# An attention and MLP stack on one core: placing side work by a running clock, summing heads on PE for the first chunk, and starting the first attention early

## Chip, core and metric

One Trainium2 chip (trn2), one core. The metric is the device time of one execution in microseconds (us). Where kernels are compared, the ratio is the mean time of one kernel's fast runs over that of the kernel before in the same rounds, so it is not quite the ratio of the medians quoted.

Engine names: PE does matmuls, DVE is the vector engine, ACT the scalar engine, POOL the general engine, SP issues DMAs. PEld is PE's loading of weights.

Words used below: a unit of a projection, of WO or of W1 is eight matmuls of 128x512, about 1.73 us. A hole is a time in which PE stands idle; the profile shows it as a bracket behind the group that ends it. The granted clock is a share of PE's full clock; below 1.00 it is called cold here.

## The reference

S = 2048 rows of D = 1024, in bfloat16; two layers, each of an attention block and an MLP block with residuals.

```python
def _A_ref(x, wqkv, wo):              # H = 32 heads of 32; each row sees 8 rows, 2 apart
    qkv = (x @ wqkv)...               # q, k, v
    idx = pos[:, None] - arange(8) * 2
    logits = einsum("bhsd,bhswd->bhsw", q, k[idx]) * scale   # masked where idx < 0
    o = einsum("bhsw,bhswd->bhsd", softmax(logits), v[idx])
    return o @ wo
def _B_ref(x, w1, b1, w2, b2):        # F = 3584
    return gelu(x @ w1 + b1) @ w2 + b2

x = x + _A_ref(_layernorm(x)); x = x + _B_ref(_layernorm(x))     # twice
```

## The kernel before

The rows are cut into four chunks of 512, so two layers make eight chunk passes, called chunks 0 to 7 here. A pass goes: first layer norm (LN1) with PE transposes, Q, K and V projections, products q times shifted k on DVE, head sum by a matmul with a 0/1 matrix, softmax, broadcast of the weights back over the head's rows by matmul, PV (weights times shifted v) on DVE, WO with residual, second layer norm (LN2), W1 with gelu, W2 with residual. A chunk's attention runs beside the W1 and W2 of the chunk before it. Chunk 0 has no such neighbour.

The parts concerned, with cuts marked by `# ...` (the other comments are mine):

```python
q8 = const.tile([P, 8, C], BF, name="q8")       # one buffer each for q, k, v, weights, output
v8 = const.tile([P, 8, KROW], BF, name="v8")    # KROW = 14 rows of halo + 512
# ...
class QK:                                       # DVE: product, then running sum over dl
    def step(self, dl):
        prod = prodp.tile([P, W, C], BF, name="prod")
        nc.vector.tensor_tensor(out=prod, in0=q8[:, dl, :]..., in1=window(k8, dl), op=ALU.mult)
        if self.acc is None: self.acc = prod
        else: nc.vector.tensor_tensor(out=self.acc, in0=self.acc, in1=prod, op=ALU.add)
# ...
def pv():
    for dl in range(8):                         # all eight steps in one piece
        t = prodp.tile([P, W, C], BF, name="prod")
        nc.vector.tensor_tensor(out=t, in0=attn4, in1=window(v8, dl), op=ALU.mult)
        # three halving additions, the last one into o8[:, dl, :]
# ...
def wo_ln(i, tail_units):                       # LN2 transposes b(st), LNB_LAG = 3 counts later
    for it in seq:
        if it[0] == "wo":
            wo_unit(wt, xt, it[1], it[2])
            if it[2] == 1:
                last = a(it[1]); pend.append((cnt + LNB_LAG, it[1]))
        else: it[1]()
        cnt += 1
        while pend and pend[0][0] <= cnt: b(pend.pop(0)[1])
# ...
for n, u in enumerate(us):                      # chunk 0's projections, LN1 of chunk 1 at the front
    u()
    if n < ST: b1u(n)
red(); exp(); bc(0); bc(1); pv()                # chunk 0's attention
for u in qkv_units(1, xa.pop(1), None): u()     # all of chunk 1's projections
xb[0], last = wo_ln(0, [])                      # nothing beside chunk 0's LN2
# ...
side = {pr: [red], pe: [exp], p0: [lambda: bc(0)], p1: [lambda: bc(1), pv]}
```

The order of the program is only a priority: the compiler's scheduler orders each engine's instructions by it, from its own estimate of when inputs are ready.

## Time and profile before

| | before |
|---|---|
| median | 1337.57 us (4 runs, 1335.61 to 1339.78) |
| span of the profiled run | 1335.4 us |
| PE busy | 1278.9 us (96%) |
| DVE busy | 805.6 us (60%) |

PE is nearly always busy, so the profile is read by its holes: the last column of the PE timeline, idle time in brackets with what ended it. The prediction shows those lines. The shares by engine of the chain of waits that ended last:

```profile
PE 81%; DVE 10%; DMA 4%; POOL 3%; ACT 1%; issue 1%; POOLq 0%; SPq 0%; ACTq 0%
```

Only about half of the 10% of DVE is PV: that of chunk 0 gives 30 us and that of chunk 1 gives 34. From the DVE and POOL timelines (start, duration, engine, line, operation), the first and last piece of that PV and the halo copy after it:

```profile
78.39 4.50 DVE L260 TENSOR_TENSOR prod<-attn,v 128x4096 bf16<-128x4096 bf16 x2 [4.62 <-ACT attn L254]
...
111.93 0.76 DVE L263 TENSOR_TENSOR o<-prod 128x512 bf16<-128x512 bf16 x2
...
108.67 4.16 POOL L182 COPY v<-v 128x112 bf16<-128x112 bf16 x1 [46.69 <-DVE prod L260]
```

The reader should see that PV occupies DVE from 78.4 to 112.7, and that nothing in WO of chunk 0 or V of chunk 1 can pass it. In the chain of waits, the last V eviction before the long hole's end waits for the halo copy.

### The profile page before, as it was taken

The numbers are of one execution on the slowest core, as the hardware profiler recorded it, in microseconds if no ns is written. First come the engines' busy times: TensorE is split into PE (matmuls) and PEld (weight loads), VectorE is DVE, ScalarE is ACT, GpSimd is POOL, SyncE is SP. The second block draws the span as 40 slices with busy tenths as digits, with TensorE's granted clock in tenths as the row PEclk, the third lists the DMA queues.
The fourth block names the chain that finished last, engine by engine and source line by source line (L and its number), as shares of the span: only waits on it lengthen the run. The fifth ranks groups of instructions, "written<-read, shape, count | busy, mean of one in ns | idle before, by whom it ended". The sixth has DMA issues, their size and how long they took to land.

```text
span 1335.4 us, 18271 instructions
## 1 busy us (share of the span) xinstructions
PE 1278.9 (96%) x8064; PEld 828.5 (62%) x8064; DVE 805.6 (60%) x836; ACT 402.9 (30%) x648; POOL 191.2 (14%) x196
## 2 busy tenths in 40 slices
PE   6996899699999999999999999999999999999998
PEld 4663358555487655966469564785648765487477
DVE  6885967586573955559374691928739284574001
ACT  3341342033610344113531235202361034501310
POOL 3002300142011310023001420004201020003000
PEclk9998899899999999999999999999999999999999
DMA  8333354344555355463455534635444526453560
GB/s 291 136 112 115 111 141 144 108 144 168 164 156 179 110 203 142 142 241 114 140 143 180 191 119 157 164 132 186 165 144 132 205 79 213 119 174 128 180 166 32
DMA packets 186912, 202.77 MB, mean 152 GB/s; under 512 B 5456, under 2 KB 152912, under 8 KB 185808
## 3 DMA queue, kind: packets, MB, share of 16 engines
q1 hardware_dynamic: 186832, 201.60, 47.1%
q8 instruction: 63, 1.03, 0.3%
q14 instruction: 17, 0.14, 0.0%
HBM read 193.21 MB, written 8.39 MB: 151 GB/s over the span
## 4 chain that ended last, share of the span: by engine, by line
PE 81%; DVE 10%; DMA 4%; POOL 3%; ACT 1%; issue 1%; POOLq 0%; SPq 0%; ACTq 0%
PE ps L315 29%; PE ps L339 28%; PE ps L187 21%; DVE prod L260 3%; DVE stats L145 2%; DMA xmid<-xt 2%; PE ps L270 1%; PE pa L163 1%; DMA xt<-xmid 1%; DVE prod L261 1%; POOL rstd L150 1%; DVE xt L273 1%; DVE xn L152 1%; DMA out_dram<-xt 1%; POOL xt L325 1%; DVE prod L262 1%
## 5 line engine op out<-in xcount | busy, mean ns | idle before, releaser
L339 PE MATMUL ps<-wt,h 128*128 128x256 bf16 x3584 | 399.6, 273 | 10.3 <-DVE xt L342 10.3
L315 PE MATMUL ps<-xnT,wt 128*128 128x512 bf16 x1792 | 393.2, 380 | 0.3 <-ACT xnT L165 0.3
L339 PEld LDWEIGHTS <-h 128*128 128x128 bf16 x3584 | 350.4, 98 | 53.5 <-issue 10.9
L187 PE MATMUL ps<-xnT,wt 128*128 128x512 bf16 x1536 | 339.3, 382 | 11.1 <-ACT v L188 11.1
L315 PEld LDWEIGHTS <-wt 128*128 128x128 bf16 x1792 | 174.3, 98 | 213.7 <-issue 8.6
L187 PEld LDWEIGHTS <-wt 128*128 128x128 bf16 x1536 | 219.4, 144 | 124.5 <-issue 17.2
L318 ACT ACTIVATE h<-ps,b1t 128x512 bf16<-128x512 f32 x224 | 152.8, 689 | 197.5 <-PE ps L315 197.4
L165 ACT ACTIVATE xnT<-pa 128x512 bf16<-128x512 f32 x128 | 69.5, 595 | 442.4 <-PE pa L163 442.3
L342 DVE TENSOR_TENSOR xt<-ps,xt 128x512 bf16<-128x512 f32 x64 | 42.9, 688 | 258.7 <-PE ps L339 258.7
L260 DVE TENSOR_TENSOR prod<-attn,v 128x4096 bf16<-128x4096 bf16 x64 | 143.6, 2286 | 87.7 <-ACT attn L254 87.7
L200 DVE TENSOR_TENSOR prod<-q,k 128x4096 bf16<-128x4096 bf16 x64 | 152.3, 2409 | 6.3 <-ACT k L188 6.3
L205 DVE TENSOR_TENSOR prod<-prod 128x4096 bf16<-128x4096 bf16 x56 | 128.0, 2285 | 0.5
L270 PE MATMUL ps<-wt,o 128*128 128x512 bf16 x512 | 114.4, 379 | 0.0
L149 POOL TENSOR_SCALAR rstd<-mv 128x1 f32<-128x1 f32 x64 | 34.2, 535 | 497.3 <-DVE mv L147 496.8
L145 DVE BATCH_NORM_STATS2 stats<-xt 128x6 f32<-128x512 bf16 x128 | 84.7, 677 | 5.0 <-DMA xt<-in_A_x_dram 2.6
L270 PEld LDWEIGHTS <-o 128*128 128x128 bf16 x512 | 49.4, 98 | 55.1
L182 POOL COPY v<-v 128x112 bf16<-128x112 bf16 x6 | 24.9, 4155 | 374.3 <-DVE prod L260 374.3
L261 DVE TENSOR_TENSOR prod<-prod 128x2048 bf16<-128x2048 bf16 x64 | 75.3, 1219 | 0.0
L325 POOL TENSOR_TENSOR xt<-xt,b2bc 128x1024 bf16<-128x1024 bf16 x32 | 70.0, 2186 | 20.5 <-DVE xn L152 20.5
L163 PE MATMUL pa<-ident,xn 128*128 128x128 bf16 x512 | 43.4, 230 | 28.2 <-DVE xn L152 16.3
L188 ACT ACTIVATE v<-ps 128x512 bf16<-128x512 f32 x64 | 37.9, 597 | 86.0 <-PE ps L187 69.3
L163 PEld LDWEIGHTS <-xn 128*128 128x128 bf16 x512 | 34.6, 103 | 42.9 <-DVE xn L152 36.5
(49 smaller groups left out, 440.4 us busy)
## 6 DMA issues: line engine op xcount, KB each, us to landing
wt<-in_B_w_dram SPq DMA_DIRECT2D x64, 1792.0 KB, 8.1
wt<-in_A_wqkv_dram SPq DMA_DIRECT2D x24, 2048.0 KB, 8.6
wt<-in_A_wo_dram SPq DMA_DIRECT2D x8, 2048.0 KB, 7.8
xmid<-xt SPq DMA_DIRECT2D x4, 1024.0 KB, 10.5
xt<-xmid SPq DMA_DIRECT2D x4, 1024.0 KB, 5.5
out_dram<-xt SPq DMA_DIRECT2D x4, 1024.0 KB, 9.8
xt<-in_A_x_dram SPq DMA_DIRECT2D x3, 1024.0 KB, 7.0
xt<-in_A_x_dram SPq DMA_DIRECT2D x4, 256.0 KB, 3.5
```

The lines of the kernel that those rows point to most:

```text
L145: nc.vector.bn_stats(out=stats[:, hh, :], in_=xt[:, st, hh * 512:(hh + 1) * 512])
L163: nc.tensor.matmul(pt[:, j, :], lhsT=xn[:, kk * P:(kk + 1) * P], rhs=ident, start=True, stop=True)
L187: nc.tensor.matmul(pt, lhsT=ws[:, kk, dl, :], rhs=xnT[:, kk, :], start=(kk == 0), stop=(kk == KT - 1))
L200: ins = nc.vector.tensor_tensor(out=prod, in0=q8[:, dl, :].unsqueeze(1).to_broadcast([P, W, C]), in1=window(k8, dl), op=ALU.mult)
L205: nc.vector.tensor_tensor(out=self.acc, in0=self.acc, in1=prod, op=ALU.add)
L260: nc.vector.tensor_tensor(out=t, in0=attn4, in1=window(v8, dl), op=ALU.mult)
L261: nc.vector.tensor_tensor(out=t[:, 0:4, :], in0=t[:, 0:4, :], in1=t[:, 4:8, :], op=ALU.add)
L270: nc.tensor.matmul(pt, lhsT=o8[:, dl, st * P:(st + 1) * P], rhs=wt[:, dl, hf * 512:(hf + 1) * 512], start=(dl == 0), stop=(dl == 7))
L315: nc.tensor.matmul(pt, lhsT=wt[:, kk, j * P:(j + 1) * P], rhs=xnT[:, kk, :], start=(kk == 0), stop=(kk == KT - 1))
L318: nc.scalar.activation(out=h, in_=pt, func=AF.Gelu_apprx_tanh, bias=b1t[:, f:f + 1])
L325: nc.gpsimd.tensor_tensor(out=xt[:, st, :], in0=xt[:, st, :], in1=b2bc, op=ALU.add)
L339: nc.tensor.matmul(pt[:, s2, :], lhsT=hs[f][:, st * P:(st + 1) * P], rhs=wt[:, f, :], start=(f == 0), stop=(f == FT - 1))
```

## The change

The intent: give every piece of side work a time on a running clock instead of a position in a list of units; start chunk 0's attention while its V projection runs; take the head sum of chunk 0 off DVE by accumulating it in PSUM; cut PV into eight separately placed steps; put LN2's transposes four projection units after their input; keep three of chunk 1's V units back to stand beside chunk 0's LN2. The core of the diff, cut (lines with `@@` and the comment in it are mine):

```diff
-POS_RED, POS_EXP, POS_BC0, POS_BC1 = 6, 10, 15, 18
-LNB_LAG = 3
+T_MM = 1.73
+T_W2 = 6.13
+A_RED, A_EXP, A_BC0, A_BC1, A_PV, A_PVSTEP = 2.0, 8.0, 16.0, 19.5, 23.0, 4.3
+LNB_LAG = 5.0
@@ class QK
-            if self.acc is None:
+            if self.on_pe:
+                self.acc = prod            # red_pe(dl): eight matmuls, start=dl==0, stop=dl==7
+            elif self.acc is None:
@@ att_units
-        def pv():
-            for dl in range(8):
+        def pv(dl):
@@ new: Clock.at(t, fn), Clock.run(fn, dur): fn placed in front of the first unit starting at t or later
+    def sched_att(i, qk, t_ready):
+        red, exp, bc, pv = att_units(i, qk)
+        clk.at(t_ready + A_RED, red)
+        clk.at(t_ready + A_EXP, exp)
+        clk.at(t_ready + A_BC0, lambda: bc(0))
+        clk.at(t_ready + A_BC1, lambda: bc(1))
+        for dl in range(8):
+            clk.at(t_ready + A_PV + A_PVSTEP * dl, (lambda d: (lambda: pv(d)))(dl))
+    def run_wo(i, res):
+        ...
+            res["last"] = a(st)
+            clk.at(clk.t + 6.9, (lambda s_: (lambda: b(s_)))(st))
+    def sched_ln1(i, t0, lag=LNB_LAG):     # a(st) at t0 + 2.5 st, b(st) lag later
@@ prologue
+    qks[0] = QK(on_pe=True)
+    us0[0](); clk.t += T_MM
+    xts[1] = load_x(1)
+    xa[1] = sched_ln1(1, clk.t, 10.0)
+    for u in us0[1:]:
+        clk.run(u, T_MM)
+    sched_att(0, qks.pop(0), 16 * T_MM + 4.5 - 8.0)
+    for u in us1[:21]:
+        clk.run(u, T_MM)
+    clk.flush(1e9)
+    run_wo(0, r)
+    for u in us1[21:]:
+        clk.run(u, T_MM)
@@ loop (cut)
+        sched_att(j + 2, qks.pop(j + 2), clk.t + 2.0)
```

More of the change, by code (lines that the diff above doesn't have):

```diff
@@ L192, in load_qkv, with reduce_heads, __init__ @@
         return wt.rearrange("p k (m e) -> p k e m", e=8)
+    def reduce_heads(lg, src, start, stop):
+        for wh in range(2):
+            for sb in range(4):
+                nc.tensor.matmul(lg[wh][32 * sb:32 * sb + 32, :, :], lhsT=sel4,
+                                 rhs=src[:, wh * 4:(wh + 1) * 4, sb * P:(sb + 1) * P],
+                                 start=start, stop=stop, tile_position=(0, 32 * sb))
     class QK:
-        def __init__(self):
+        def __init__(self, on_pe=False):
             self.acc = None
+            self.on_pe = on_pe
+            self.lg = None
         def step(self, dl):
@@ L206, in step, with red_pe, u @@
             return ins
+        def red_pe(self, dl):
+            src = self.acc
+            def u():
+                if self.lg is None:
+                    self.lg = [pslg.tile([P, 4, P], F32, name="lg") for _ in range(2)]
+                reduce_heads(self.lg, src, dl == 0, dl == 7)
+            return u
     def att_units(i, qk):
@@ L212, in red @@
         def red():
-            acc = qk.acc
-            lg = [pslg.tile([P, 4, P], F32, name="lg") for _ in range(2)]
-            for wh in range(2):
-                for sb in range(4):
-                    nc.tensor.matmul(lg[wh][32 * sb:32 * sb + 32, :, :], lhsT=sel4,
-                                     rhs=acc[:, wh * 4:(wh + 1) * 4, sb * P:(sb + 1) * P],
-                                     start=True, stop=True, tile_position=(0, 32 * sb))
+            if qk.on_pe:
+                lg = qk.lg
+            else:
+                lg = [pslg.tile([P, 4, P], F32, name="lg") for _ in range(2)]
+                reduce_heads(lg, qk.acc, True, True)
             lgs = smx.tile([P, W, P], F32, name="lgs")
@@ L255, in bc @@
                                      func=AF.Copy)
-        def pv():
-            for dl in range(8):
-                t = prodp.tile([P, W, C], BF, name="prod")
-                nc.vector.tensor_tensor(out=t, in0=attn4, in1=window(v8, dl), op=ALU.mult)
-                nc.vector.tensor_tensor(out=t[:, 0:4, :], in0=t[:, 0:4, :], in1=t[:, 4:8, :], op=ALU.add)
-                nc.vector.tensor_tensor(out=t[:, 0:2, :], in0=t[:, 0:2, :], in1=t[:, 2:4, :], op=ALU.add)
-                nc.vector.tensor_tensor(out=o8[:, dl, :], in0=t[:, 0, :], in1=t[:, 1, :], op=ALU.add)
+        def pv(dl):
+            t = prodp.tile([P, W, C], BF, name="prod")
+            nc.vector.tensor_tensor(out=t, in0=attn4, in1=window(v8, dl), op=ALU.mult)
+            nc.vector.tensor_tensor(out=t[:, 0:4, :], in0=t[:, 0:4, :], in1=t[:, 4:8, :], op=ALU.add)
+            nc.vector.tensor_tensor(out=t[:, 0:2, :], in0=t[:, 0:2, :], in1=t[:, 2:4, :], op=ALU.add)
+            nc.vector.tensor_tensor(out=o8[:, dl, :], in0=t[:, 0, :], in1=t[:, 1, :], op=ALU.add)
         return red, exp, bc, pv
@@ L273, in wo_unit @@
         nc.vector.tensor_tensor(out=xs, in0=pt, in1=xs, op=ALU.add)
-    def wo_ln(i, tail_units):
-        xt = xts[i]
-        wt = load_w(A_wo.rearrange("(m e) n -> m e n", e=8), 8, D)
-        xnT, a, b = ln_units(xt)
-        main = []
-        for st in range(ST):
-            main.append(("wo", st, 0))
-            main.append(("wo", st, 1))
-        pend = []
-        cnt = 0
-        last = None
-        seq = main + [("tail", u) for u in tail_units]
-        for it in seq:
-            if it[0] == "wo":
-                wo_unit(wt, xt, it[1], it[2])
-                if it[2] == 1:
-                    last = a(it[1])
-                    pend.append((cnt + LNB_LAG, it[1]))
-            else:
-                it[1]()
-            cnt += 1
-            while pend and pend[0][0] <= cnt:
-                b(pend.pop(0)[1])
-        for _, st in pend:
-            b(st)
-        return xnT, last
     def w1_units(xnT, hs):
@@ L360, in u @@
                         qk.step(dl)
+                        if qk.on_pe:
+                            clk.at(clk.t + T_MM + 2.7, qk.red_pe(dl))
                 else:
@@ L372, in qkv_units @@
         return us
-    xa = {0: ln_all(xts[0])}
-    xts[1] = load_x(1)
-    late_consts()
-    qks = {0: QK(), 1: QK()}
-    us = qkv_units(0, xa.pop(0), qks[0])
-    xnT1, a1, b1u = ln_units(xts[1])
-    for st in range(ST):
-        a1(st)
-    for n, u in enumerate(us):
-        u()
-        if n < ST:
-            b1u(n)
-    xa[1] = xnT1
-    red, exp, bc, pv = att_units(0, qks[0])
-    red(); exp(); bc(0); bc(1); pv()
-    late_bias()
-    for u in qkv_units(1, xa.pop(1), None):
-        u()
@@ L392, with __init__, at, flush @@
-    xb = {}
-    xb[0], last = wo_ln(0, [])
-    first_qk = None
+    class Clock:
+        def __init__(self):
+            self.t = 0.0
+            self.q = []
+            self.n = 0
+        def at(self, t, fn):
+            self.q.append((t, self.n, fn))
+            self.n += 1
+            self.q.sort(key=lambda e: (e[0], e[1]))
+        def flush(self, t):
+            while self.q and self.q[0][0] <= t:
+                self.q.pop(0)[2]()
+        def run(self, fn, dur):
+            self.flush(self.t)
+            fn()
+            self.t += dur
@@ new lines @@
+    clk = Clock()
+    def sched_att(i, qk, t_ready):
[7 more added lines that the diff above has]
+    def run_wo(i, res):
+        xt = xts[i]
+        wt = load_w(A_wo.rearrange("(m e) n -> m e n", e=8), 8, D)
+        xnT, a, b = ln_units(xt)
+        res["xnT"] = xnT
+        for st in range(ST):
+            for hf in range(2):
+                clk.run(lambda: wo_unit(wt, xt, st, hf), T_MM)
+            res["last"] = a(st)
+            clk.at(clk.t + 6.9, (lambda s_: (lambda: b(s_)))(st))
@@ new lines, in sched_ln1 @@
+    def sched_ln1(i, t0, lag=LNB_LAG):
+        xnT, a, b = ln_units(xts[i])
+        for st in range(ST):
+            clk.at(t0 + 2.5 * st, (lambda s_: (lambda: a(s_)))(st))
+            clk.at(t0 + 2.5 * st + lag, (lambda s_: (lambda: b(s_)))(st))
+        return xnT
+    xa, xb, qks = {}, {}, {}
+    wq0 = None
+    xa[0] = ln_all(xts[0])
+    late_consts()
+    qks[0] = QK(on_pe=True)
+    us0 = qkv_units(0, xa.pop(0), qks[0])
+    us0[0]()
+    clk.t += T_MM
+    xts[1] = load_x(1)
+    xa[1] = sched_ln1(1, clk.t, 10.0)
@@ L395 @@
+    for u in us0[1:]:
+        clk.run(u, T_MM)
+    sched_att(0, qks.pop(0), 16 * T_MM + 4.5 - 8.0)
+    late_bias()
+    us1 = qkv_units(1, xa.pop(1), None)
+    for u in us1[:21]:
+        clk.run(u, T_MM)
+    clk.flush(1e9)
+    r = {}
+    run_wo(0, r)
+    for u in us1[21:]:
+        clk.run(u, T_MM)
+    clk.flush(1e9)
+    xb[0] = r["xnT"]
+    qks[1] = QK()
     for dl in range(8):
         ins = qks[1].step(dl)
-        if first_qk is None:
-            first_qk = ins
-    tc.add_manual_dep(first_qk.ins, last.ins.name,
-                      mybir.DependencyInfo(mybir.DependencyClass.NoSync, mybir.DependencyReason.DATA),
-                      reason="keep the first LN2 chain free of filler work")
+        if dl == 0:
+            tc.add_manual_dep(ins.ins, r["last"].ins.name,
+                              mybir.DependencyInfo(mybir.DependencyClass.NoSync, mybir.DependencyReason.DATA),
+                              reason="keep the first LN2 chain free of filler work")
@@ L403 @@
+    sched_att(1, qks.pop(1), clk.t + 36.0)
     for j in range(N):
         hs = []
-        w1u = w1_units(xb.pop(j), hs)
-        side = {}
-        if j + 1 < N:
-            red, exp, bc, pv = att_units(j + 1, qks.pop(j + 1))
-            pr, pe, p0, p1 = (22, 26, 28, 29) if j == 0 else (POS_RED, POS_EXP, POS_BC0, POS_BC1)
-            side = {pr: [red], pe: [exp], p0: [lambda: bc(0)], p1: [lambda: bc(1), pv]}
-        w2u = w2_units(hs, xts[j])
-        main = w1u + w2u
-        have_ln1 = j + 2 < N
@@ L414 @@
-        if have_ln1:
-            xts[j + 2] = load_x(j + 2)
-        lnst = {}
-        early_wo = (j + 2 >= N and j + 1 < N)
-        for n, u in enumerate(main):
-            if n == FT:
-                add_b2(xts[j])
-            if early_wo and n == FT + 5:
-                xb[j + 1], _ = wo_ln(j + 1, main[n:])
-                break
-            u()
-            for s in side.pop(n, []):
-                s()
-            if have_ln1 and n >= FT and n - FT < ST:
-                if n == FT:
-                    lnst["x"], lnst["a"], lnst["b"] = ln_units(xts[j + 2])
-                st = n - FT
-                lnst["a"](st)
-                if st > 0:
-                    lnst["b"](st - 1)
-            if have_ln1 and n == FT + ST:
-                lnst["b"](ST - 1)
@@ L436 @@
-        assert not side, side
-        store_x(j, xts.pop(j))
-        if have_ln1:
-            xa[j + 2] = lnst["x"]
-            qks[j + 2] = QK()
-            xb[j + 1], _ = wo_ln(j + 1, qkv_units(j + 2, xa.pop(j + 2), qks[j + 2]))
+        xj = xts[j]
+        t_w1 = clk.t
+        clk.at(t_w1 + 3.0, lambda: add_b2(xj))
+        for u in w1_units(xb.pop(j), hs):
+            clk.run(u, T_MM)
+        w2u = w2_units(hs, xj)
+        if j + 2 < N:
+            xts[j + 2] = load_x(j + 2)
+            xa[j + 2] = sched_ln1(j + 2, clk.t + 2.0)
@@ new lines @@
+        early_wo = (j + 2 >= N and j + 1 < N)
+        r = {}
+        for n, u in enumerate(w2u):
+            if early_wo and n == 5:
+                clk.flush(1e9)
+                run_wo(j + 1, r)
+            clk.run(u, T_W2)
+        store_x(j, xts.pop(j))
+        if j + 2 < N:
+            run_wo(j + 1, r)
+            qks[j + 2] = QK()
+            for u in qkv_units(j + 2, xa.pop(j + 2), qks[j + 2]):
+                clk.run(u, T_MM)
+            sched_att(j + 2, qks.pop(j + 2), clk.t + 2.0)
@@ L445 @@
+        if j + 1 < N:
+            xb[j + 1] = r["xnT"]
+    clk.flush(1e9)
 _INS = ['A_x', 'A_wqkv', 'A_wo', 'B_x', 'B_w1', 'B_b1', 'B_w2', 'B_b2']
```

## The prediction

> **What bounds the kernel now.** I read the page's busy table first, then the PE timeline for the places where PE is idle, then the waits, then the table of stretches for the price of an idle time beyond its own length.
>
> The busy table of the page:
>
> ```profile
> PE 1278.9 (96%) x8064; PEld 828.5 (62%) x8064; DVE 805.6 (60%) x836; ACT 402.9 (30%) x648; POOL 191.2 (14%) x196
> ```
>
> PE is busy 1278.9 of 1335.4 us; only 56.5 us can be won without removing PE work, and DVE (805.6) bounds nothing on average, only in places. The PE timeline, whose last column is the idle time before a group and its releaser:
>
> ```profile
> 9.91 1.03 PE L163 MATMUL pa<-ident,xn 128*128 128x128 bf16 x8 [9.91 <-POOL rstd L150]
> ...
> 16.93 3.62 PE L187 MATMUL ps<-xnT,wt 128*128 128x512 bf16 x8
> 20.34 1.06 PE L163 MATMUL pa<-ident,xn 128*128 128x128 bf16 x8
> ...
> 24.28 39.88 PE L187 MATMUL ps<-xnT,wt 128*128 128x512 bf16 x184
> 64.09 0.61 PE L217 MATMUL lg<-prod,sel 128*32 128x512 bf16 x8
> ...
> 113.50 9.22 PE L187 MATMUL ps<-xnT,wt 128*128 128x512 bf16 x32 [11.12 <-ACT v L188]
> ...
> 143.60 1.03 PE L163 MATMUL pa<-ident,xn 128*128 128x128 bf16 x8 [5.37 <-DVE xn L152]
> 144.90 41.69 PE L315 MATMUL ps<-xnT,wt 128*128 128x512 bf16 x184 [0.26 <-ACT xnT L165]
> ...
> 245.93 1.22 PE L339 MATMUL ps<-wt,h 128*128 128x256 bf16 x5 [10.29 <-DVE xt L342]
> ...
> 261.06 7.07 PE L270 MATMUL ps<-wt,o 128*128 128x512 bf16 x32
> ...
> 276.57 3.62 PE L187 MATMUL ps<-xnT,wt 128*128 128x512 bf16 x16
> 281.47 0.62 PE L163 MATMUL pa<-ident,xn 128*128 128x128 bf16 x8 [1.27 <-DVE xn L152]
> ```
>
> The reader should see three kinds of hole. First, chunk 0's attention: the head reduction starts at 64.09, PV fills DVE from 78.4 to 112.7, and chunk 1's V projection may not overwrite the single v8 buffer before PV and the halo copy have read it (11.12 us); then chunk 0's second layer norm has nothing beside it (5.37 us). Second, in the first W2, eight PV steps in one priority block keep DVE from emptying W2's PSUM tiles (10.29 us). Third, after each WO phase the fourth layer-norm transpose stands two projection units behind, too soon (1.27 us here). The first two waits are single events. The same third wait recurs at 435.5/440.9, 595.0/600.5, 754.6/760.1, 914.2/920.2, 1074.2/1078.7 and 1212.6, with 0.2 plus 0.35 to 1.9 us each time; adding all brackets after 270 us gives 8.85 us.
>
> The table of stretches (us; busy times; then PE clock, DMA share, GB/s):
>
> ```profile
> 113.50:122.70 9.20, 9.20 (x33) 4.86 (x33) 0.00 (x0) 3.21 (x6) 0.00 (x0) 0.76 0.01 2
> 248.00:261.00 13.00, 13.00 (x108) 11.06 (x106) 0.82 (x2) 0.72 (x2) 0.00 (x0) 0.88 0.01 1
> 420.60:580.00 159.40, 157.96 (x1010) 102.88 (x1008) 100.19 (x104) 50.30 (x81) 21.07 (x22) 1.00 0.50 159
> ```
>
> After each long hole PE runs at a granted clock of 0.76 and 0.88, so a hole costs more than its length. A steady chunk has 1.44 us of PE idle in 159.4: there is almost nothing to win from chunk 2 on, other than the third kind of hole.
>
> **What the Trainium skill says.** "TensorE: Matmul & The Clock Gate", Part 1, says an idle PE falls to half clock and needs about one window (3.4 us) of work to come back. The trace agrees: 32 matmuls after the 11.12 us hole took 9.22 us, where 32 cost 32 x 0.216 = 6.92 at full clock (2.3 us lost); the W2 units after the second hole lost about 2.4. The same page, Part 3, says matmuls in different column groups run side by side: the eight reduction matmuls take 0.55 us (64.09 to 64.64), not 8 x 0.216 = 1.73, so moving the head sum to PE is cheap. "VectorE: DVE Perf Modes", tier table, caps a bf16 tensor-tensor at two elements a cycle: 4096 elements measure 2.29 us, 0.56 ns each, so neither the product nor the accumulation gets cheaper, and only removing the additions helps. "PSUM — Partial Sum Buffer", the four rules, forbids two accumulation groups open together in one bank and quadrant; here each of the two reduction tiles has its own bank and four groups in four quadrants. No run yet shows that.
>
> **The change part by part.**
>
> *Chunk 0's head sum on PE.* It removes 7 additions x 2.285 = 16 us from DVE and adds 64 - 8 = 56 matmuls: 7 groups x 0.55 = 3.9 us of PE time. DVE was not yet the limit (its last addition ended at 61.8, before PE's 64.1), so the sum as such wins nothing; it lets the reduction follow the last K projection instead of the end of V.
>
> *First projection.* x of chunk 1 is loaded behind Wq and Wk, and its layer norm is spread over the projection. Before, 28 of its 32 transposes stood in a block from 20.34 to 24.28 (3.9 us, paced by ACT); spread, four groups at 0.45 to 0.5 cost 2.0. The first projection can start when the last normalised x of chunk 0 is out of PSUM (15.45) instead of 16.93.
>
> *New clock of the prologue, an estimate from the rows above.* Start 15.5; first unit cold 3.45 -> 18.95; 15 units x 1.731 (39.8/23) = 26.0, transposes 2.0, six reduction groups 3.3 -> last K at 50.2; eviction and last product 0.6 + 2.3 plus place in the queue -> reduction done at 54.5. Before, the reduction ended at 64.7 and PV began at 78.4, 13.7 later; so PV begins near 68.2 and, at 34.3 us for eight steps, ends near 102.5 (it was 112.7). PE meanwhile: eight V units 13.85 and two reduction groups 1.1 -> 65.2; eight broadcasts 2.7 and 21 units of chunk 1 (36.35) -> 104.3. So PE arrives at WO just after PV has ended and the 11.12 us vanish. V unit n of chunk 1 follows PV step n by more than 7 us, so the single v8 is no wait either. WO takes 13.85, the three V units kept back 5.2, transposes 1.35 -> 124.7; in the old trace the fourth normalised x came 4.85 us after the end of WO, now at about 123.9, so the 5.37 us close too. Last transposes and eviction 1.3: W1 starts near 126.0 instead of 144.90. **Gain 18.9 us.** Cross-check: holes 16.5, cold loss 2.3, transposes 1.9, start 1.4, small gaps near 1 make 23.1, less 3.9 new PE work: 19.2.
>
> *First W1 and W2.* PV is cut into eight steps placed between W2 units, so an eviction waits for one step at most and four PSUM tiles cover that. The 10.29 us, a broadcast gap of 0.56 and the cold 2.4 go: 13.2. But the second broadcast still stands behind W2's second unit, at W1 start + 62.6; PV starts at +65.1, needs 34.3 and gives way to five evictions x 0.69: it ends near +103, where PE reaches WO at about +102.4 (W1 48.4, W2 49.0, reduction 0.55, broadcasts 2.6, transposes 1.8). I charge 1 us for that. **Gain 12.2.**
>
> *Layer-norm transposes four units behind instead of two or three.* Four units are 6.9 us against the 4.85 measured: all 8.85 us of the third kind should go. Against it, in W2 the transposes of the next chunk's layer norm now fall three groups to one unit boundary (offsets 5, 7.5, 10 against units of 6.13 us) with two PSUM tiles between PE and ACT: I charge 0.25 x 6 = 1.5. **Gain 7.3.**
>
> *Steady attention.* Reduction, exponential and broadcasts come some 6 us earlier in W1. The last sum on DVE ended 1.6 us after the projection (321.5 against 319.9); the reduction now stands about 5 us after it: no wait, no gain, as PV ended 30 us before WO.
>
> Sum: 18.9 + 12.2 + 7.3 = 38.4; 1337.6 - 38.4 = 1299.2, rounded to **1300 us**. Floor: busy PE 1278.9 + 3.9 - 4.7 cold - 2 transposes = 1276, with head and tail idle of 11.3 + 6.1 and 2.2 between span and time: 1296.
>
> **The rivals.** (a) *PV remains late*: if PE reaches WO before PV has ended, the hole only moves from V to WO. For it: my two times differ by 2 us, and the compiler's order, made without the chip, already sends the fourth transpose too early by up to 1.9 us. Against it: the V units kept back. It makes 1304 to 1310. (b) *The new reduction holds PE*: each group waits for a product, in an in-order queue; if the products are 1 us late eight times, 8 us return: 1308. Against it: DVE has 2.3 us of product and 1 of layer norm to do in a 4.3 us pair of units. (c) *DVE becomes the bound of the first W2* as evictions and PV compete, PE waiting 3 to 6 us at WO: 1303 to 1306. (d) *The holes were hidden anyway*: the chain of waits speaks against it, as PE carries 81% of it and no other engine could hold the end. It would be 1335.
>
> **Range and chances.** The gains are bounded by 1296 below; the rivals cost 4 to 10 each and one of them may well come in part, so 1293 to 1311. Two per cent is 1310.8, so both (a) and (b) would be needed in full to miss it: faster 0.86, within 2% 0.13, slower 0.01.
>
> **What would show it.** Right: PE busy about 1277 with idle near 20; 64 + 56 reduction matmuls; chunk 0's PV starting near 68 and ending near 103; first W1 near 126; first WO of chunk 1 about 103 us after that; no bracket over 1 us after WO. Wrong: a bracket over 3 us before chunk 0's WO (rival a), brackets by DVE products before the reduction groups (b), one before chunk 1's WO (c), or brackets by ACT inside the transposes of W2. A steady chunk well off 158 us would refute the third part.

## The result, and the profile after

The changed kernel takes 1296.66 us (median of 8, 1296.25 to 1298.34), the kernel before 1337.38 (12 runs); the ratio is 0.9697, interval 0.9688 to 0.9707. That is 3.0% faster; 1300 was predicted, range 1293 to 1311.

The busy table and the shares of the chain:

```profile
PE 1273.6 (98%) x8120; PEld 826.9 (64%) x8120; DVE 786.4 (61%) x829; ACT 401.0 (31%) x648; POOL 166.4 (13%) x196
...
PE 94%; DVE 3%; DMA 1%; ACT 0%; POOL 0%; SPq 0%; issue 0%; DVEq 0%; ACTq 0%
```

PE's share of the chain went from 81 to 94%. The 56 added matmuls (8120 - 8064) are those of the head sum. PE's idle is now 1294.9 - 1273.6 = 21.3 us, of which 9.68 at the head and about 6 at the tail were there before. The PE timeline, from the first projection to WO of chunk 1:

```profile
14.79 8.67 PE L189 MATMUL ps<-xnT,wt 128*128 128x512 bf16 x32 [0.20 <-ACT xnT L167]
...
28.80 0.62 PE L199 MATMUL lg<-prod,sel 128*32 128x512 bf16 x8 [0.76 <-DVE prod L211]
...
55.58 0.62 PE L199 MATMUL lg<-prod,sel 128*32 128x512 bf16 x8
...
66.64 0.39 PE L269 MATMUL lg<-at,efull 32*128 32x512 bf16 x2
...
70.57 0.39 PE L269 MATMUL lg<-at,efull 32*128 32x512 bf16 x2
...
103.77 1.46 PE L289 MATMUL ps<-wt,o 128*128 128x512 bf16 x6
107.41 9.36 PE L289 MATMUL ps<-wt,o 128*128 128x512 bf16 x42 [2.19 <-DVE o L282]
...
127.98 38.15 PE L307 MATMUL ps<-xnT,wt 128*128 128x512 bf16 x176 [0.78 <-ACT xnT L167]
...
176.97 6.28 PE L331 MATMUL ps<-wt,h 128*128 128x256 bf16 x56
...
229.70 10.52 PE L289 MATMUL ps<-wt,o 128*128 128x512 bf16 x48
```

Against the lines of before: the 11.12 us hole in V is gone and a 2.19 us hole before WO stands in its place; the 5.37 us hole of LN2 is gone; W1 starts at 127.98 instead of 144.90; the 10.29 us hole in W2 is gone; after 300 us there is no bracket at all. On DVE, the end of chunk 0's softmax and the first and last piece of its PV:

```profile
64.04 1.23 DVE L261 TENSOR_TENSOR at<-lgs,t 128x1024 bf16<-128x1024 f32 x1
73.39 4.50 DVE L279 TENSOR_TENSOR prod<-attn,v 128x4096 bf16<-128x4096 bf16 x2 [8.13 <-ACT attn L274]
...
106.93 0.76 DVE L282 TENSOR_TENSOR o<-prod 128x512 bf16<-128x512 bf16 x2
```

PV is earlier than before (78.4 to 112.7), but it stands 8.13 us idle behind the softmax. The spans split at two landmarks, the first W1 and chunk 1's WO:

| stretch | before, us | after, us | won | predicted |
|---|---|---|---|---|
| start to first W1 | 144.90 | 127.98 | 16.9 | 18.9 |
| first W1 to chunk 1's WO | 116.16 | 101.72 | 14.4 | 12.2 |
| chunk 1's WO to the end | 1074.34 | 1065.20 | 9.1 | 7.3 |
| sum | 1335.4 | 1294.9 | 40.5 | 38.4 |

The total came out within 2 us of the forecast because three misses of about 2 us each partly cancelled; that is in part luck. The experiments ask which term was off in each.

### The profile page after: what moved, and what is told of

Its sections match the earlier page's. It is cut to its first block, busy times and chain, and to the rows that moved or that the text cites. A ratio compares the mean times of both kernels' runs of the same rounds, so it can differ in the third digit from the quotient of the medians.

```text
span 1294.9 us, 18380 instructions
## 1 busy us (share of the span) xinstructions
PE 1273.6 (98%) x8120; PEld 826.9 (64%) x8120; DVE 786.4 (61%) x829; ACT 401.0 (31%) x648; POOL 166.4 (13%) x196
## 4 chain that ended last, share of the span: by engine, by line
PE 94%; DVE 3%; DMA 1%; ACT 0%; POOL 0%; SPq 0%; issue 0%; DVEq 0%; ACTq 0%
PE ps L331 30%; PE ps L307 30%; PE ps L189 22%; PE ps L289 8%; PE pa L165 2%; DVE prod L279 1%; DMA wt<-in_A_wqkv_dram 1%; DVE prod L280 1%; PE lg L199 1%; DVE prod L281 0%; DVE prod L211 0%; PE lg L269 0%; DVE stats L147 0%; POOL rstd L151 0%; DVE o L282 0%; ACT attn L274 0%
## 5 line engine op out<-in xcount | busy, mean ns | idle before, releaser
L211 DVE TENSOR_TENSOR prod<-q,k 128x4096 bf16<-128x4096 bf16 x64 | 148.4, 2340 | 13.5 <-ACT k L190 13.5
L218 DVE TENSOR_TENSOR prod<-prod 128x4096 bf16<-128x4096 bf16 x49 | 112.0, 2286 | 0.5
L151 POOL TENSOR_SCALAR rstd<-mv 128x1 f32<-128x1 f32 x64 | 25.9, 406 | 574.4 <-DVE mv L149 569.9
L190 ACT ACTIVATE k<-ps 128x512 bf16<-128x512 f32 x64 | 38.2, 597 | 71.4 <-PE ps L189 71.4
L190 ACT ACTIVATE q<-ps 128x512 bf16<-128x512 f32 x64 | 38.3, 598 | 67.6 <-PE ps L189 67.6
L154 DVE TENSOR_SCALAR xn<-xt,mv,rstd 128x1024 bf16<-128x1024 bf16 x64 | 35.0, 547 | 34.8 <-POOL rstd L152 34.7
## 6 DMA issues: line engine op xcount, KB each, us to landing
xmid<-xt SPq DMA_DIRECT2D x4, 1024.0 KB, 10.8
```

The source lines that it names most:

```text
L190: nc.scalar.activation(out=dst[:, dl, off:off + C], in_=pt, func=AF.Copy)
L211: ins = nc.vector.tensor_tensor(out=prod, in0=q8[:, dl, :].unsqueeze(1).to_broadcast([P, W, C]), in1=window(k8, dl), op=ALU.mult)
```

## Experiments

Eleven kernels ran, all correct. The kernel before was timed in the same rounds and stayed between 1337.46 and 1338.06. Theory: three separate kinds of PE hole, closed one by one. Rivals: time closed in one place comes back in another, or a given part of the change does nothing.

### The later LN2 transposes alone

```diff
 # kernel before, wo_ln; "lag" replaces LNB_LAG at its one use
+        lag = 5 if len(tail_units) == 24 else LNB_LAG
```

> The kernel before with one thing changed: after WO the layer-norm transposes stand four projection units behind instead of two. If the third kind of hole is a wait for a transpose queued too soon, all brackets after WO but those of the last chunk go: 1337.4 less about 8.5 = 1329. Rival: the time comes back elsewhere in the chunk because DVE or ACT finishes late anyway: 1336 to 1337.

Measured: 1326.04 us, ratio 0.9913 (0.9900 to 0.9927): 11.6 us by ratio, more than expected. All brackets between chunk 1's WO and the end but one (0.16 us) are gone, so nothing came back elsewhere. From chunk 1's WO (259.87 here) to the end of the span of 1323.4 it takes 1063.5 us instead of 1074.3, that is 10.8 won where the removed brackets sum to 8.69. The PE timeline of the kernel before shows where the other 2 us were:

```profile
427.86 3.62 PE L270 MATMUL ps<-wt,o 128*128 128x512 bf16 x16
431.31 0.61 PE L163 MATMUL pa<-ident,xn 128*128 128x128 bf16 x8
```

Sixteen matmuls are drawn as 3.62 us, but the next group starts 3.45 us after them: a drawn end reaches 0.17 us into what follows. When PE stops, that 0.17 us is counted as busy, and the bracket is too short by it. Twelve brackets were removed: 8.69 + 12 x 0.17 = 10.7. A cold clock is no rival here: the stretches of a steady chunk, shown further down, have 1.00 before and after. The Trainium skill's page "Perfetto Trace Analysis", on the tensor engine instruction, says that the profiler estimates the end of a matmul rather than observing it; the 0.17 us agrees.

### The split PV of the first W2 alone

```diff
 # kernel before; pv takes a list of steps
+            if j == 0:
+                side[p1] = [lambda: bc(1), lambda: pv([0])]
+                for n_, ds in ((30, [1]), (31, [2, 3]), (32, [4]), (33, [5, 6]), (34, [7])):
+                    side[n_] = [(lambda d: (lambda: pv(d)))(ds)]
```

> The kernel before with only the first W2's PV cut into five pieces placed between W2 units. My theory: the 10.3 us hole in W2 goes with the cold clock after it, 1337.4 less 12 to 14 = 1324. Rival (DVE is the bound of that stage, evictions and PV add up): PV ends later and PE waits at WO instead, so only 4 to 8 us are won: 1329 to 1333.

(The edit makes six pieces; the text says five.) Measured: 1324.54 us, ratio 0.9901 (0.9887 to 0.9914), 13.2 us, the size predicted for the hole with its cold clock. Chunk 1's WO starts at 248.13, 103.2 us after the first W1, with no bracket in front:

```profile
144.92 41.45 PE L315 MATMUL ps<-xnT,wt 128*128 128x512 bf16 x184 [0.26 <-ACT xnT L165]
...
195.49 6.28 PE L339 MATMUL ps<-wt,h 128*128 128x256 bf16 x56
...
248.13 7.07 PE L270 MATMUL ps<-wt,o 128*128 128x512 bf16 x32
```

So DVE was not the bound of that stage; only the order of its work was.

### Chunk 0's head sum back on DVE

```diff
-    qks[0] = QK(on_pe=True)
+    qks[0] = QK(on_pe=False)
```

> The changed kernel with only chunk 0's head sum put back on DVE (seven additions, one reduction). Theory: the reduction comes some 8 us later, PV ends 5 to 8 us later and the hole before WO grows by that plus the 3.9 us of PE work saved; in sum 4 to 8 us slower than 1296.7: 1301 to 1305. Rival: DVE was not the limit there, so only the 3.9 us of PE work return: 1293.

Measured: 1299.60 us, ratio 0.9715 against 0.9697 for the whole change: about 2.4 us slower, less than the 4 to 8 expected, with the sign of the theory. The intervals of the two ratios just touch (0.9702 to 0.9728, 0.9688 to 0.9707), but no single run of one lies among those of the other. PE timeline:

```profile
64.67 0.62 PE L199 MATMUL lg<-prod,sel 128*32 128x512 bf16 x8
...
104.52 5.34 PE L289 MATMUL ps<-wt,o 128*128 128x512 bf16 x24
113.04 7.04 PE L289 MATMUL ps<-wt,o 128*128 128x512 bf16 x24 [3.18 <-DVE o L282]
```

The reduction is 9 us later (some 8 were expected), yet the hole grew only from 2.19 to 3.18: PE does 24 WO matmuls before it stops, not 6. Twenty-four is four PSUM tiles times six of eight contraction steps, which fits PV's last two outputs being the ones missing; that reading is inferred from the count. The longer hole cost clock as well: 24 matmuls at 0.216 plus 0.17 are 5.4 us, and took 7.04. Summing on PE is thus worth 2 to 3 us, in spite of its 3.9 us of extra matmuls.

### Chunk 0's two groups of broadcasts together

```diff
-    sched_att(0, qks.pop(0), 16 * T_MM + 4.5 - 8.0)
+    sched_att(0, qks.pop(0), 16 * T_MM + 4.5 - 8.0, bc0=16.0, bc1=16.1)
 # bc0, bc1 stand in for A_BC0, A_BC1
```

> The changed kernel with chunk 0's second group of broadcast matmuls queued right behind the first instead of two projection units later. Theory: PV began 5 us later than predicted because of the place of the second broadcast in PE's queue; it will start near 70.5 instead of 73.4, the 2.2 us hole before WO goes, 1296.7 less 2 to 2.5 = 1294.4. Rival: the halo copy on POOL holds PV (it reads the halo): PV's start and the time stay, 1296.7.

Measured: 1296.46 us, ratio 0.9692 (0.9678 to 0.9705): no change, the rival's number, but not for the rival's reason. The PE timeline:

```profile
67.25 0.39 PE L269 MATMUL lg<-at,efull 32*128 32x512 bf16 x2
67.25 0.39 PE L269 MATMUL pa<-at,efull 32*128 32x512 bf16 x2
...
68.48 0.37 PE L269 MATMUL lg<-at,efull 32*128 32x512 bf16 x1 [0.26 <-ACT attn L274]
...
69.16 0.38 PE L269 MATMUL lg<-at,efull 32*128 32x512 bf16 x1
...
69.85 0.38 PE L269 MATMUL pa<-at,efull 32*128 32x512 bf16 x1
...
70.53 0.38 PE L269 MATMUL pa<-at,efull 32*128 32x512 bf16 x1
...
106.09 10.52 PE L289 MATMUL ps<-wt,o 128*128 128x512 bf16 x48
```

The hole before WO did go, and PV started at 71.97 instead of 73.39. But the gain was spent: the second four broadcasts, now waiting for PSUM tiles that ACT frees one at a time, ran singly between projection matmuls. A broadcast and the projection matmul after it took 0.69 us together (69.16 to 69.85), where that matmul alone takes 0.22, and four broadcasts queued together take 0.33 (66.64 to 66.97 in the changed kernel). With the 0.26 us wait, PE needs 1.7 us more from the first broadcast to WO (38.84 against 37.13). Another 0.6 us is that this profiled run was later by so much already at the first broadcast (67.25 against 66.64), before the edit acts. WO is reached at 106.1 instead of 103.8 and the first W1 at 127.83 instead of 127.98. The place of the broadcasts does move PV; putting them together is not the way to use it.

### No V units kept back

```diff
-    for u in us1[:21]:
+    for u in us1[:24]:
 # and us1[24:], nothing, after WO
```

> The changed kernel with all 24 projection units of chunk 1 queued before chunk 0's WO, none kept back. Theory: the 2.2 us hole before WO goes (WO comes 5.2 us later), but chunk 0's second layer norm has nothing beside it again and shows the old bracket of about 5.4 us plus a cold start of W1: 1296.7 - 2.2 + 6 = about 1300.5. Rival: the keeping back does nothing that the rest does not: 1294.5.

Measured: 1301.21 us, ratio 0.9726: as the theory had it, about 4 us slower. WO shows no hole, and LN2's is back:

```profile
109.13 10.52 PE L289 MATMUL ps<-wt,o 128*128 128x512 bf16 x48
...
129.45 1.03 PE L165 MATMUL pa<-ident,xn 128*128 128x128 bf16 x8 [4.12 <-DVE xn L154]
130.74 39.85 PE L307 MATMUL ps<-xnT,wt 128*128 128x512 bf16 x176 [0.26 <-ACT xnT L167]
```

The cold start of W1 is back too: its first 176 matmuls take 39.85 us, against 38.15 in the changed kernel.

### Steady attention at its old place

```diff
-            sched_att(j + 2, qks.pop(j + 2), clk.t + 2.0)
+            sched_att(j + 2, qks.pop(j + 2), clk.t + 8.4)
```

> The changed kernel with the attention of chunks 2 to 7 queued 6.4 us later in W1, about where the kernel before had it. Theory: PV still ends long before WO, so nothing changes: 1296 to 1297.5. Rival: the earlier attention is part of the steady gain: 1299 or more.

Measured: 1297.83 us, ratio 0.9700 against 0.9697: nothing, as expected. A steady chunk, from WO to WO, takes 158.04 us (388.43 to 546.47) against 158.05 in the changed kernel. The median is 0.3 us outside the range written down; the ratio and the chunk decide.

### LN1's transposes spread over W2

```diff
-            xa[j + 2] = sched_ln1(j + 2, clk.t + 2.0)
+            xa[j + 2] = sched_ln1(j + 2, clk.t + 2.0, T_W2, T_W2)
 # new last argument: the step between row tiles, 2.5 by default
```

> The changed kernel with the next chunk's layer-norm transposes in W2 spread to one group per W2 unit. A steady chunk of the changed kernel takes 158.05 us, of the kernel before with the later transposes 157.63. Theory: the difference is PE broken into short pieces by the transposes that fall together at one unit boundary; spread, a chunk takes 157.6, six chunks win 2.5 us: 1294.2. Rival: the difference comes from the attention's place in W1 (seen in the run with late attention instead): 1296.7 here.

Measured: 1294.71 us, ratio 0.9677 (0.9662 to 0.9691), between 2 and 2.7 us faster than the change. The stretch table, one steady chunk from WO to WO (us, then busy time of PE, PEld, DVE, ACT, POOL with counts, PE clock, DMA share, GB/s), of the kernel before, the first experiment, the changed kernel and this one in turn:

```profile
420.48:579.90 159.42, 157.98 (x1010) 102.89 (x1008) 100.19 (x104) 50.30 (x81) 21.07 (x22) 1.00 0.50 159
```

```profile
417.50:575.12 157.62, 157.62 (x1010) 103.15 (x1008) 99.31 (x104) 50.08 (x81) 19.05 (x22) 1.00 0.50 161
```

```profile
545.77:703.82 158.05, 158.03 (x1011) 103.12 (x1008) 99.89 (x105) 50.05 (x81) 23.33 (x22) 1.00 0.50 160
```

```profile
387.53:545.16 157.63, 157.63 (x1011) 103.04 (x1009) 99.60 (x104) 50.09 (x81) 19.04 (x22) 1.00 0.50 161
```

The changed kernel's chunk is 0.42 us longer than need be, with PE shown busy throughout. Its PE timeline inside W2 shows how:

```profile
507.96 0.38 PE L165 MATMUL pa<-ident,xn 128*128 128x128 bf16 x4
508.18 0.38 PE L331 MATMUL ps<-wt,h 128*128 128x256 bf16 x2
508.45 0.38 PE L165 MATMUL pa<-ident,xn 128*128 128x128 bf16 x4
```

Three groups of transposes fall to one unit boundary and W2 matmuls are pushed in two at a time; that the groups wait for the two PSUM tiles of transposes is read from the code, not shown. From 507.34 to 509.74 four half groups and ten W2 matmuls take 2.40 us; at the normal rates of 0.45 per group of eight and 0.109 per W2 matmul (6.11/56) they are 2.0. No bracket shows it, because each piece's drawn end covers the stop.

### Chunk 1's LN1 moved beside chunk 0's V

```diff
-    xa[1] = sched_ln1(1, clk.t, 10.0)
+    xa[1] = sched_ln1(1, 16 * T_MM)
```

> The changed kernel with chunk 1's first layer norm moved from the middle of chunk 0's Q and K projections to beside its V projections. Theory: the chain last K, reduction, softmax, PV, WO sets the hole before WO; without 1.8 us of transposes and 1.2 us of waits for products in front of the last K, PV ends about 3 us sooner and the 2.2 us hole goes: 1294 to 1295. Rival: something later in the chain (V, halo copy, broadcasts' place) holds PV: 1296.7.

Measured: 1297.89 us, ratio 0.9701: nothing won, my theory of that chain falls, the rival stands. PE timeline of this run, with the end of the softmax from DVE's:

```profile
53.30 0.62 PE L199 MATMUL lg<-prod,sel 128*32 128x512 bf16 x8
...
66.17 0.39 PE L269 MATMUL lg<-at,efull 32*128 32x512 bf16 x2
...
108.58 9.36 PE L289 MATMUL ps<-wt,o 128*128 128x512 bf16 x42 [2.58 <-DVE o L282]
```

```profile
62.09 1.22 DVE L261 TENSOR_TENSOR at<-lgs,t 128x1024 bf16<-128x1024 f32 x1
```

The reduction came 2.3 us earlier and the softmax ended at 63.3 instead of 65.3, but the first broadcast stayed at 66.2: it stands behind the V units in PE's queue. The second four stood at 71.35 and PV began at 74.57, later than in the changed kernel. So it is the broadcasts' place, not the softmax, that starts PV.

### Chunk 1's LN1 in a block at the front, as before

```diff
+    xts[1] = load_x(1)                # ahead of the weights
     late_consts()
-    xa[1] = sched_ln1(1, clk.t, 10.0)
+    xa[1], a1, b1u = ln_units(xts[1])
+    for st in range(ST):
+        a1(st)
+        clk.at(T_MM * (st + 1), (lambda s_: (lambda: b1u(s_)))(st))
```

> The changed kernel with chunk 1's x loaded before the weights and its layer norm in a block at the start of the first projection, as the kernel before had it. Theory: the first projection starts near 16.9 instead of 14.8 and 1.9 us of transposes paced by ACT come on top, less 1.2 us of waits for products: PV ends 2 to 3 us later, 1298.5 to 1299.5. Rival: the start is hidden behind the chain to PV: 1296.7.

Measured: 1301.13 us, ratio 0.9722, about 3.3 us slower than the change by ratio, a little above the range given. The last reduction ends at 58.5 and the first W1 starts at 130.40, 2.4 later than in the changed kernel. The profiled run was the fastest of its four (1299.06), at a mean clock of 1.000 and inside the range given; the other three took some 2 us more at 0.997 to 0.998. Their traces were not kept, but the repeat of the changed kernel below shows such a spread.

### A version from the findings, and the change again

Three edits on the changed kernel: the spread of LN1 above; chunk 1's LN1 beside chunk 0's V; and chunk 0's attention registered while V is still running, the broadcasts 10.4 and 14.6 after its start.

```diff
-    xa[1] = sched_ln1(1, clk.t, 10.0)
+    xa[1] = sched_ln1(1, 16 * T_MM - 3.0)
-    for u in us0[1:]:
+    for n, u in enumerate(us0[1:]):
+        if n == 17:
+            sched_att(0, qks.pop(0), 28.6, bc0=10.4, bc1=14.6, pv0=18.6)
         clk.run(u, T_MM)
```

> The changed kernel with layer-norm transposes spread over W2, chunk 1's first layer norm beside chunk 0's V projections, and chunk 0's broadcasts queued one unit ahead of the end of V (first four) and two units later (last four). Theory: the run with the late layer norm left PV where it was because the broadcasts stood behind V in PE's queue; with them moved too, PV starts near 71 and ends near 105, the hole before WO shrinks to under 0.5: 2.4 for the spread and about 2 for the hole, 1292.5. Rival: the halo copy, which needs the last V, holds PV: 1294.7, the value of the spread alone.

> The changed kernel unaltered, on the same chip and in the same rounds as the two others, as their measure: 1296.5 to 1297.5.

Measured in the same rounds: 1292.33 us (1291.52 to 1292.57), ratio 0.9657, against 1297.38 (1296.90 to 1298.17), ratio 0.9697, for the change unaltered. It beats both. From its DVE and PE timelines:

```profile
71.47 4.50 DVE L279 TENSOR_TENSOR prod<-attn,v 128x4096 bf16<-128x4096 bf16 x2 [7.60 <-ACT k L190]
```

```profile
64.36 0.39 PE L269 MATMUL lg<-at,efull 32*128 32x512 bf16 x2
...
68.30 0.39 PE L269 MATMUL lg<-at,efull 32*128 32x512 bf16 x2
...
105.48 9.36 PE L289 MATMUL ps<-wt,o 128*128 128x512 bf16 x41 [0.81 <-DVE o L282]
```

With the first broadcast moved to 64.4, PV starts at 71.5 and the hole before WO is 0.81. The halo copy of v ended at 67.85, ahead of that, so it does not hold PV. The bracket of PV names an eviction of k: the last copy of the weights ended at 70.96 and that eviction, next on ACT, at 71.45. Why PV waited for it was not looked into. The hole is a little over the 0.5 expected. The edits were run together. By the traces, 1.9 of the 5 us lie before the first W1 (126.05 instead of 127.98); the spread's 2 to 2.7 us come after it. The two prologue edits were not separated.

The repeat's profiled run was its slowest (1298.17 us). Weight loads, matmuls and stretches at the hole before WO, the last line from the first run of the changed kernel:

```profile
103.40 1.18 PEld L289 LDWEIGHTS <-o 128*128 128x128 bf16 x6
```

```profile
103.62 1.24 PE L289 MATMUL ps<-wt,o 128*128 128x512 bf16 x5
107.26 11.05 PE L289 MATMUL ps<-wt,o 128*128 128x512 bf16 x42 [2.40 <-DVE o L282]
```

```profile
107.26:111.00 3.74, 3.74 (x11) 1.40 (x12) 1.67 (x3) 0.00 (x0) 0.00 (x0) 0.62 0.00 0
```

```profile
107.41:111.00 3.59, 3.59 (x17) 1.58 (x18) 2.73 (x5) 0.00 (x0) 0.00 (x0) 1.00 0.00 0
```

Six weight loads stand before the stop but five matmuls, so one record is missing and the 2.40 is the old hole of 2.19: from the first WO matmul to the restart both runs take 3.64 us. Yet here the 42 matmuls run at a cold clock and take 1.7 us longer. The same hole thus costs clock in one execution and not in another. The two other runs of the change above 1298 (1298.03 and 1298.34) also have a mean clock of 0.997, so a difference of under 2 us between two of these kernels can be this alone.

## Why the prediction was right, and where it was off

- **PE holes bound the kernel, and two of the three kinds close for good.** Shown: the first two experiments close one kind each and nothing comes back; the rival that the holes were hidden (1335) is refuted.
- **Start to first W1, 18.9 predicted, 16.9 measured.** Right: first projection at 14.8 (15.5 predicted), PE at WO at 103.8 (104.3), LN2's hole closed by the units kept back (the experiment without them). It closed narrowly: the fourth normalised x was ready at 126.52 and its transposes began at 126.59. The "4.85 us after the end of WO" was misread: it is the time from the end of the third transposes in chunk 1's WO; in chunk 0 that time was 5.5 us. Wrong: "PV begins near 68.2". The step that failed is the carrying over of 13.7 us from reduction to PV. It measured 73.39 - 56.1 = 17.3 (the reduction was 1.6 us late besides), because the broadcasts sit at unit boundaries in PE's queue: the first waited 1.4 us after the softmax had ended and the second stood two projection units further back. The late layer norm and the combined version show that the place decides. So the hole moved in part from V to WO: rival (a), 2.19 us of it, made milder because six matmuls of WO need no late output.
- **Eight broadcasts at 2.7 us.** Mis-sized: queued in fours they take 0.33 us per four, 0.66 in all. I had read the price from chunk 0 of the kernel before, where they ran singly.
- **The head sum on PE.** Its 3.9 us hold (seven more groups of eight at 0.55), and so does that it lets the attention start early: undone, the reduction is 9 us later and the kernel 2 to 3 us slower. "The sum as such wins nothing" was not tested, as no run sums on PE in the kernel before. The prediction's rule from "PSUM — Partial Sum Buffer" is narrower on the page: two accumulation groups open in one bank and quadrant may not both begin with a matmul that clears. The groups here all begin so, but lie apart, and every run was correct. Rival (b), products holding the reduction, came to 0.76 + 0.46 = 1.2 us.
- **First W1 to WO, 12.2 predicted, 14.4 measured.** The 13.2 for the hole was right on its own (13.2 measured). The 1 us charged for PV's end did not occur: WO starts at 229.70 with no bracket, while PV's last output ends at 230.7. Rival (c) is refuted. The step that failed is one left out of the sum: W1 began cold after LN2's hole, so closing that hole also shortened W1. With only PV split, the stretch takes 103.2 us, W1's part of it 195.49 - 144.92 = 50.6. In the changed kernel W1 takes 176.97 - 127.98 = 49.0, and the remainder is the same within 0.1. The run without the kept-back units brings the slow start back.
- **Chunk 1's WO to the end, 7.3 predicted, 9.1 measured.** Right in mechanism. The term "8.85 us of brackets" was too small: 10.8 measured, by the 0.17 us that each bracket leaves out. The charge for transposes falling together, 0.25 us a chunk, was too small as well: 0.42, in the five chunks of this stretch. (Its offsets count from 2 us into W2, so the three groups come at 7, 9.5 and 12, before the boundary at 12.26.) With the last chunk's bracket, 10.8 + 0.3 - 5 x 0.42 gives 9.0.
- **Steady attention earlier, no gain.** Shown by the run that puts it back.
- **The floor of 1296 us** was not one: the combined version, which only moves work, reached 1292.33.

## What to carry to other kernels

When the bounding engine is nearly full, list its holes, price each with the cold clock after it, and ask for each whether the work behind it waits for data or only stands in the wrong place of a queue; the two look alike in a busy table. Count a hole from the start of one group to the start of the next, not by the idle bracket, since the drawn end of a matmul covers part of every stop, and compare the counts of matmuls and weight loads, since a missing record makes a hole look longer. When work is moved, check what it is queued with: here four narrow matmuls together cost no more than one alone.

## What the Trainium skill lacked or had wrong

- "TensorE: Matmul & The Clock Gate", Part 3, has narrow tiles running side by side, but not what happens when they are released one at a time: four broadcasts of 32 rows took 0.33 us queued together, but singly each took 0.69 us with the projection matmul after it, which alone takes 0.22.
- The same page's practical rule is to avoid idle gaps over about 3 us. Here a shorter hole could cost clock too: the same 2.19 us cost none in one run of the changed kernel (42 matmuls in 9.36 us) and 1.7 us in its repeat (42 in 11.05). A hole of 2.58 us cost none in the run with the late layer norm (42 in 9.36), and one of 3.18 us did (24 in 7.04). The page calls its activity window free-running, which may be why two runs differ, but a gap of 2.19 us does not fill a window of some 3.4 us; the cause stays open.
- "Perfetto Trace Analysis" says that a matmul's end is estimated, but gives no size for what that hides: 0.17 us per stop here, 2 of 10.8 us in the first experiment.
- No page has that transposes falling together in the middle of other matmuls can cost PE time without any idle time shown: 0.42 us per chunk.
